# One decode step of attention and a squared-relu block: query tiles of 512 columns, output weights on VectorE, the bias behind the transposition

## The chip, the cores and the metric

The kernel runs on one core of a Trainium2 chip. The metric is the device time of one execution in microseconds, taken as the median of several runs. The kernel before ran at 1052.48 us (median of 3 runs, 1052.36 to 1053.69).

## What is computed

One token x of 640 values passes an attention block and a dense block, both modulated by a condition c:

```python
mod = (silu(c) @ w_mod)                      # six vectors: sa, ca, ga, sb, cb, gb
h = layernorm(x) * (1 + ca) + sa
q = (h @ wq)                                  # 32 heads of 192
p = softmax(q @ k_cache^T / sqrt(192))        # 8192 positions for each head
x = x + ga * ((p @ v_cache) @ wo)             # wo: 6144 x 640
h = layernorm(x) * (1 + cb) + sb
x = x + gb * (relu(h @ w1 + b1)**2 @ w2 + b2) # w1: 640 x 1536, w2: 1536 x 640
```

All is float32. The two caches are 403 MB of the 452 MB that are read, and each value is used once.

## The kernel before

The heads go in 16 pairs. A pair's keys come in three parts of 8192 values for each of the 128 partitions (64 positions a partition), its values in three parts of the same size. `ring` holds three slots; one transfer fills a slot with a part of keys (first half) and the part of values that is two parts older (second half). SyncE's queue is the order of all transfers: `l0` (the weights of the first modulation, the query weights of pairs 0 to 2, small columns), `l1` (query weights of pairs 3 to 10), `c0` and `c1` (the first key parts and the last query weights), 46 transfers of `stream`, and then `c48` (output weights of pairs 0 to 3 and values), `wob` (output weights of pairs 4 to 7), `wos` (of pairs 8 to 15), `c49` (the last values), `wm1`, `w1`, and `w2` in four pieces. `issue(n)` (lines 486 to 498) sends a transfer when the slot's keys are done (`tk_free`, from VectorE) and its values are done (`values_done`, from TensorE).

Ahead of the loops TensorE computes the query rows (lines 260 to 301): a round is up to four pairs, each pair's 384 columns in its own 32 rows of a PSUM bank, 5 contraction blocks. ScalarE copies them to `qr` (`keep_rows`). For each pair `act_stage` picks one pair's row into `stage`, a product with `ones` spreads it over all partitions (`pe_query`), and ScalarE copies that to `qb`.

Each engine then runs a loop of its own over the pairs. VectorE (`dve_pair`) multiplies a part of keys by the query in place, sums most of it, and finds the maximum; GpSimd adds the halves of the rest (line 385); ScalarE takes the exponential; TensorE (line 326) turns the pair's outputs before (`pe_turn`, line 324), multiplies values by probabilities in three steps of 16 units ("va", "vb", "vc"), spreads the next query between the first two, and sums the probabilities. TensorE's loop is created with `head_slot={ET.PE: 0}`: its first instruction is put at the start of a block of instruction memory.

Behind the loops VectorE multiplies the turned outputs by the output weights and adds them to `acc` (`attend`, line 449, three instructions of 640 columns for a pair) for pairs 0 to 13. It waits for `c48` (pairs 0 to 3), `wob` (4 to 7) and `wos` (8 and on). `project` (line 386) scales the last pair's outputs, head by head; `ON_DVE` is 14, so pair 13 comes behind the second head. TensorE takes pairs 14 and 15 itself, into `ps_att` (`pe_attend`, line 554), and then adds the sum of `acc` over the partitions to the same bank (line 570). The rest is one chain: gate and residual (lines 576, 577), layer norm with the second modulation's weights `wm1` between its steps on TensorE (line 193, called at 574, 580 and 585), a transposition (587), w1 (597), a transposition of the result (604), squared relu (605), w2 (615), gate, residual, and the transfer of the result. w1's bias enters ahead of w1 as four products with the identity (589); three more products with the identity (591) follow and their result isn't used.

Of the kernel before, what the change touches and what calls it, by code (L numbers as in the profile page):

```python
# [4 lines left out]
AF = mybir.ActivationFunctionType  # L5
ALU = mybir.AluOpType
# [3 lines left out]
P = 128  # L10
# [33 lines left out]
WM = KB * 3 * D  # L44
W2_CUT = (6 * D, 9 * D, 11 * D, FB * D)
GROUP = 4
ON_DVE = 14
EPS = 1e-5


# [47 lines left out]
        self.n = 0  # L98


def block_kernel(nc, l0, l1, c0, c1, stream, c48, wob, wos, c49, wm1, w1, w2, out):
    sem = nc.alloc_semaphore
    V, A, L, T, S = (Line(nc, e, n) for e, n in ((nc.vector, "dve"), (nc.scalar, "act"), (nc.gpsimd, "pool"),
                                                 (nc.tensor, "pe"), (nc.sync, "sp")))
# [11 lines left out]
    def sb(name, *shape):  # L116
        return nc.alloc_sbuf_tensor(name, [P, *shape], F32)
# [6 lines left out]
    ident, ones, mean = sb("ident", P), sb("ones", P), sb("mean", P)  # L124
    mask, quad, eps_t = sb("mask", E), sb("quad", NV), sb("eps_t", 1)
    small, e_t, h1 = sb("small", SMALL), sb("silu", KB), sb("h1", KB)
    qr, stage, qb = sb("qr", len(ROUNDS), PW), sb("stage", PW), sb("qb", PW)
    ga, x_t, bbt = sb("ga", DG), sb("x_t", DG), sb("bbt", 32 * (FB + KB))
    ra, rb, rc = sb("ra", NPOS), sb("rb", ROWS), sb("rc", NPOS)
    sc = [sb(f"sc{s}", NPOS) for s in range(2)]  # L130
    mp = [sb(f"mp{s}", 1) for s in range(2)]
# [10 lines left out]
    def dma(dst, src, s):  # L142
        nc.sync.dma_start(dst, src).then_inc(s, 16)  # L143
# [102 lines left out]
    def spread(dst, src, n):  # L246
        room = om[:, :, :].rearrange("p d e -> p (d e)")[:, :32 * n]
        V.wait(V.last())
        V.wait(V.mark(v.tensor_copy(room.rearrange("p (b r) -> p b r", r=32), src[:, :, None].to_broadcast([P, n, 32]))))
        V.mark(v.transpose(dst, room))  # L250

    spread(x_t[:, :], x_c, KB)
    spread(bbt[:, :32 * FB], bbc[:, :FB], FB)
    spread(bbt[:, 32 * FB:], bbc[:, FB:], KB)
    for a in range(2):
        V.mark(v.memset(ps_o[a][:96, :], 0.0))
    V.mark(v.memset(ps_sum[:, :2], 1.0))
    m_ready = V.last()

    def query_rows(r, w, bank):  # L260
        for b in range(KB):
            for g, i in enumerate(ROUNDS[r]):
                o = pe.matmul(bank[32 * g:32 * (g + 1), :PW], h1[:, b:b + 1].to_broadcast([P, 32]),
                              w[:, g * WQ + b * PW:g * WQ + (b + 1) * PW], start=(b == 0), stop=(b == KB - 1))
        return T.mark(o)

    def keep_rows(r, bank, m):
        A.wait(m)
        n = 32 * len(ROUNDS[r])
        return A.mark(act.activation(qr[:n, r], bank[:n, :PW], AF.Copy, scale=DH ** -0.5))  # L270

    def act_stage(i):
        r = [i in pairs for pairs in ROUNDS].index(True)
        g = ROUNDS[r].index(i)
        A.wait(m_rows[r])
        return act.activation(stage[:, :], qr[:, r], AF.Copy, scale=ident[:, 32 * g:32 * g + 1])

    def pe_query():
        return pe.matmul(ps_q[:, :PW], ones[:, :], stage[:, :], start=True, stop=True)
# [27 lines left out]
    def done(step, i):  # L307
        return T.sem, T0 + len(PE_STEPS) * i + PE_STEPS.index(step) + 1
# [13 lines left out]
    def pe_turn():  # L322
        T.take(tk_o)
        return pe.matmul(ps_oT[:, :NV], os_[:96].rearrange("p a d -> p (a d)"), quad[:96, :], start=True, stop=True)  # L324

    with nc.Fori(0, NPAIR, engines=bass.OrderedEngineSet([ET.PE]), head_slot={ET.PE: 0}):
        pe_turn().then_inc(T.sem, 1)
        pe_max(0)
        T.take(tk_c)
        T.take(tk_p[0])  # L330
        pe_values(2, range(16))
        T.take(tk_s)
        pe_query().then_inc(T.sem, 1)
# [56 lines left out]
    def project(a):  # L390
        n = 32 * NV
        return (v.scalar_tensor_tensor(om[:n], ps_o[a][:n].rearrange("p (d e) -> p d e", e=E), r2[:n, a:a + 1],  # L392
                                       mask[:n, None, :].to_broadcast([n, ED, E]), op0=ALU.mult, op1=ALU.mult),
                lambda: v.tensor_reduce(os_[:n, a], om[:n], axis=AX.X, op=ALU.add))  # L394
# [63 lines left out]

    def late_wo(i):
        group, k = divmod(i, GROUP)  # L460
        at = (slot[0], WO_AT) if group == 0 else (slot[1], 0) if group == 1 else (slot[2], (group - 2) * GROUP * WO)
        return at[0][:, at[1] + k * WO:at[1] + (k + 1) * WO]

    attended = {}
# [1 line left out]
    def attend_range(first, end, m):  # L466
        for i in range(first, end):
            attended[i] = attend(i, late_wo(i), m)
# [14 lines left out]
    def values_done(m):  # L483
        return done(("va", "vb", "vc")[m % 3], m // 3)
# [17 lines left out]
        forward(n)  # L502
        issue(n + 2)
    forward(PARTS - 1)
    S.wait((tk_free, PARTS - 1))
    dma(slot[1][:, :GROUP * WO], wob, w_sem[2])
    S.wait((tk_free, PARTS), values_done(PARTS - 3))
    dma(slot[2][:, :2 * GROUP * WO], wos, w_sem[3])
    S.wait(values_done(PARTS - 4))
    dma(slot[1][:, PART:], c49, slot_sem[1])  # L510
    forward(PARTS)

    attend_range(0, GROUP, landed(PARTS))
    attend_range(GROUP, 2 * GROUP, (w_sem[2], 16))
    V.wait(done("sum", NPAIR - 1))
    V.wait(V.mark(v.reciprocal(r2[:, :], ps_sum[:, :2])))
    for a in range(2):
        V.wait(done("vb" if a == 0 else "vc", NPAIR - 1))
        scaled, sums = project(a)
        V.wait(V.mark(scaled))  # L520
        o = sums()
        if a == 0:
            V.wait(V.mark(o))
            attend_range(2 * GROUP, ON_DVE - 1, (w_sem[3], 16))
        else:
            o.then_inc(tk_o, 1)
            attend_range(ON_DVE - 1, ON_DVE, (w_sem[3], 16))
    m_acc = attended[ON_DVE - 1]

    wm1_t, w1_t, w2_t = slot[0][:, :WM], slot[1][:, :KB * FF], slot[2][:, :FB * D]  # L530
    S.wait(done("vb", NPAIR - 1), attended[GROUP - 1])
    dma(wm1_t, wm1, w_sem[4])
    S.wait(attended[2 * GROUP - 1])
    dma(w1_t, w1, w_sem[5])
    forward(PARTS + 1)
    S.wait(attended[3 * GROUP - 1])
    a = 0
    for n, b in enumerate(W2_CUT):
        dma(w2_t[:, a:b], w2[:, a:b], w_sem[6 + n])
# [4 lines left out]
    def room(n):  # L544
        r = tail[0][:, :n]
        tail[0] = tail[0][:, n:]
        return r

    x1, gate, gb2, y, hT, cb1, xm2, sq2, h2 = (room(DG) for _ in range(9))
    f, fT = room(FG), room(FG)  # L550
    s2, ss2, sd2, rs2 = (room(1) for _ in range(4))
    ps_b, ps_f, ps_y = ps_mx[0], ps_o[0], ps_o[1]

    def pe_attend(i):
        wo = late_wo(i).rearrange("p (j n) -> p j n", j=NV)
        T.wait(turned[i])
        for j in range(NV):
            for g in range(G):
                o = pe.matmul(ps_att[32 * g:32 * (g + 1), :DG], oT[:, i, j:j + 1].to_broadcast([P, 32]),
                              wo[:, j, DG * g:DG * (g + 1)], start=i == ON_DVE and j == 0, stop=False)  # L560
        return o

    T.wait((w_sem[3], 16))
    for i in range(ON_DVE, NPAIR - 1):
        pe_attend(i)
    act_turned(NPAIR - 1, T.mark(pe_turn()))
    pe_attend(NPAIR - 1)
    T.wait(m_acc)
    for g in range(G):
        i = pe.matmul(ps_att[32 * g:32 * (g + 1), :DG], ones[:, :32], acc[:, DG * g:DG * (g + 1)], start=False, stop=True)  # L570
    m_att = T.mark(i)
    T.wait((w_sem[4], 16))
    w_b = wm1_t
# [11 lines left out]
                     lambda: mod(ps_b, w_b, 3, range(1, 3)), summed=True)  # L585
    V.wait(m_h2)
    m_hT = V.mark(v.transpose(hT, h2))
    for g in range(G):
        pe.matmul(ps_f[32 * g:32 * (g + 1), :FG], ident[:, 32 * g:32 * (g + 1)], bbt[:, :FG], start=True, stop=False)
    for _ in range(3):  # L590
        pe.matmul(ps_oT[:32, :512], ident[:, :32], bbt[:, :512], start=True, stop=True)
    T.wait(m_hT, (w_sem[5], 16))
    hT3 = hT.rearrange("p (b r) -> p b r", r=32)
    for b in range(KB):
        at = b * FF
        for g in range(G):
            i = pe.matmul(ps_f[32 * g:32 * (g + 1), :FG], hT3[:, b], w1_t[:, at + FG * g:at + FG * (g + 1)],
                          start=False, stop=(b == KB - 1))
    m_f = T.mark(i)
    V.wait(V.mark(v.tensor_copy(gate, ps_b[:, 2 * DG:3 * DG])))  # L600
    V.wait(V.mark(v.tensor_mul(gb2, gate, bbt[:, FG:])))
    m_x2 = V.mark(v.tensor_add(x1, x1, gb2))
    V.wait(m_f)
    V.wait(V.mark(v.transpose(f, ps_f[:, :FG])))
    m_fT = V.mark(v.scalar_tensor_tensor(fT, f, 0.0, f, op0=ALU.max, op1=ALU.mult))
    T.wait(m_fT)
    fT3 = fT.rearrange("p (b r) -> p b r", r=32)
    for b in range(FB):
        for n, c in enumerate(W2_CUT):
            if b * D < c:  # L610
                T.wait((w_sem[6 + n], 16))
                break
        for g in range(G):
            o = b * D + DG * g
            i = pe.matmul(ps_y[32 * g:32 * (g + 1), :DG], fT3[:, b], w2_t[:, o:o + DG], start=(b == 0), stop=(b == FB - 1))  # L615
    m_y = T.mark(i)
    V.wait(m_y, m_x2)
    V.wait(V.mark(v.tensor_mul(y, ps_y[:, :DG], gate)))  # L618
# [62 lines left out]
```

## Time and profile before

| | |
|---|---|
| median of 3 runs | 1052.48 us |
| the profiled execution | 1052.26 us, span 1050.9 us |
| VectorE busy | 868.7 us (83%) |
| TensorE matmul busy | 460.6 us (44%), 2154 matmuls |
| GpSimd busy | 193.4 us (18%) |
| ScalarE busy | 46.3 us (4%), 124 instructions |
| read from HBM | 451.82 MB, 430 GB/s over the span |

The span runs from the first to the last instruction of the execution that was profiled; its own time lies 1.4 us above it. A matmul of float32 is two passes, each with a load of weights, and the profile counts the passes. An engine that is busy for a small share of the span can still set the end if something waits for it there, so the shares are read beside the waits and the timeline.

### The profile page before, as it was taken

How to read it: one execution, taken by the hardware profiler on the slowest of the kernel's cores; microseconds unless marked ns; L12 is line 12 of the kernel's file. 1: busy time of each engine (PE TensorE's matmuls, PEld its weight loads, DVE VectorE, ACT ScalarE, POOL GpSimd, SP SyncE). 2: the span in 40 equal slices, each digit the busy share in tenths (PEclk: the TensorE clock that was granted, in tenths of full speed). 3: DMA queues.
4: the chain of work that ended last, by engine and by line, in shares of the span. 5: the costliest groups of instructions: out<-in, count | busy, mean ns of one | idle time of the engine just before them, and what ended most of it. 6: DMA issues, size and time to landing. Idle time of an engine off the chain costs nothing. (4 is left out here: it accounts for less than half of the span.)

```text
span 1050.9 us, 5797 instructions
## 1 busy us (share of the span) xinstructions
PE 460.6 (44%) x2154; PEld 142.4 (14%) x2154; DVE 868.7 (83%) x411; ACT 46.3 (4%) x124; POOL 193.4 (18%) x63
## 2 busy tenths in 40 slices
PE   1543444362543543453624434434526345344327
PEld 0211111110111111111101111111102011111103
DVE  0269999898889898998988897988988888979973
ACT  1100000000000000000000000000000000000000
POOL 1011313112122122131131121121211311311100
PEclk9966767666676666676676766666766767666759
DMA  9999999999999999999999999999999999999997
GB/s 412 417 434 440 437 437 437 434 434 417 439 437 437 437 432 437 419 437 437 437 439 427 439 424 432 437 439 437 432 434 427 429 439 437 437 437 432 421 429 333
DMA packets 8657, 451.92 MB, mean 430 GB/s; under 512 B 965, under 2 KB 969, under 8 KB 1353
## 3 DMA queue, kind: packets, MB, share of 16 engines
q1 hardware_dynamic: 8648, 451.83, 99.5%
q8 instruction: 4, 0.07, 0.0%
q14 instruction: 5, 0.03, 0.0%
HBM read 451.82 MB, written 0.00 MB: 430 GB/s over the span
## 5 line engine op out<-in xcount | busy, mean ns | idle before, releaser
L407 DVE TENSOR_TENSOR ring<-ring,qb 128x8192 f32<-128x8192 f32 x48 | 417.1, 8689 | 79.5 <-DVEq L84 79.5
L314 PE MATMUL ps_o<-ring,p 128*32 128x512 f32 x1536 | 357.9, 812 | 206.9 <-PEq L66 206.9
L385 POOL TENSOR_TENSOR ring<-ring 128x1792 f32<-128x1792 f32 x48 | 189.9, 3955 | 782.6 <-POOLq L66 782.6
L314 PEld LDWEIGHTS ps_o<-ring,p 128*32 128x32 f32 x1536 | 87.4, 144 | 453.2 <-issue 452.9
L320 PE MATMUL ps_mx<-ident,mp 128*128 128x128 f32 x64 | 24.5, 487 | 140.3 <-PEq L66 140.3
L324 PE MATMUL ps_oT<-quad,os 96*128 96x3 f32 x34 | 9.3, 344 | 169.1 <-PEq L66 169.1
L409 DVE TENSOR_REDUCE rc<-ring 128x36 f32<-128x4608 f32 x16 | 79.2, 4953 | 2.3
L409 DVE TENSOR_REDUCE ra<-ring 128x36 f32<-128x4608 f32 x16 | 79.2, 4953 | 2.3
L409 DVE TENSOR_REDUCE rb<-ring 128x72 f32<-128x4608 f32 x16 | 79.2, 4953 | 2.3
L454 DVE SCALAR_TENSOR_TENSOR acc<-ring,oT,acc 128x640 f32<-128x640 f32 x42 | 37.1, 884 | 4.9 <-DMA ring<-in_wos 2.7
L421 DVE TENSOR_REDUCE nm<-ps_mx 128x1 f32<-128x128 f32 x32 | 9.3, 291 | 34.1 <-DVEq L84 34.1
L320 PEld LDWEIGHTS ps_mx<-ident,mp 128*128 128x128 f32 x64 | 16.0, 311 | 150.6 <-issue 150.6
L324 PEld LDWEIGHTS ps_oT<-quad,os 96*128 96x128 f32 x34 | 8.3, 305 | 183.3 <-issue 183.3
L413 DVE TENSOR_REDUCE rc<-ring 128x28 f32<-128x1792 f32 x16 | 32.1, 2009 | 0.0
L413 DVE TENSOR_REDUCE ra<-ring 128x28 f32<-128x1792 f32 x16 | 32.1, 2009 | 0.0
L413 DVE TENSOR_REDUCE rb<-ring 128x56 f32<-128x1792 f32 x16 | 32.1, 2005 | 0.0
L354 ACT ACTIVATE oT<-ps_oT 128x3 f32<-128x3 f32 x16 | 2.8, 173 | 590.3 <-PE ps_oT L324 590.3
L392 DVE SCALAR_TENSOR_TENSOR om<-ps_o,r,mask 96x512 f32<-96x512 f32 x34 | 25.4, 747 | 3.8 <-PE ps_o L314 2.6
L347 ACT ACTIVATE p<-sc,nm 128x256 f32<-128x256 f32 x32 | 16.2, 508 | 185.8 <-DVE nm L421 185.8
L394 DVE TENSOR_REDUCE os<-om 96x64 f32<-96x512 f32 x34 | 23.2, 682 | 1.2
L336 PE MATMUL ps_sum<-sp,ones 128*128 128x2 f32 x32 | 8.9, 348 | 19.6 <-PEq L66 19.6
L193 PE MATMUL ps_o<-ring,silu 128*32 128x480 f32 x40 | 6.7, 837 | 23.1 <-DVE silu L186 23.1
(92 smaller groups left out, 153.8 us busy)
## 6 DMA issues: line engine op xcount, KB each, us to landing
ring<-in_c SPq DMA_DIRECT2D x2, 7936.0 KB, 48.2
ring<-in_l SPq DMA_DIRECT2D x1, 7693.5 KB, 21.2
ring<-in_l SPq DMA_DIRECT2D x1, 7680.0 KB, 38.9
ring<-in_wos SPq DMA_DIRECT2D x1, 7680.0 KB, 28.7
ring<-in_c SPq DMA_DIRECT2D x1, 5056.0 KB, 25.3
ring<-in_wm SPq DMA_DIRECT2D x1, 4800.0 KB, 36.5
ring<-in_c SPq DMA_DIRECT2D x1, 4096.0 KB, 38.1
ring<-in_wob SPq DMA_DIRECT2D x1, 3840.0 KB, 27.7
```

The source lines that it names most:

```text
L314: i = pe.matmul(ps_o[h][32 * g:32 * (g + 1), :], p_t[h][:, E * j:E * (j + 1)].rearrange("p e r -> p (e r)"), t[:, k], start=(j == 0), stop ...
L320: pe.matmul(ps_mx[s][:, :P], mp[s][:, :].to_broadcast([P, P]), ident[:, :], start=True, stop=True).then_inc(tk_x, 1)
L324: return pe.matmul(ps_oT[:, :NV], os_[:96].rearrange("p a d -> p (a d)"), quad[:96, :], start=True, stop=True)
L347: act.activation(p_t[s][:, :, :], sc[s][:, :, None].to_broadcast([P, NPOS, 32 // E]), AF.Exp, bias=nm[s][:, :], accum_out=sp[:, s:s + 1]). ...
L385: pool.tensor_add(r[:, keep:, :w], r[:, keep:, :w], r[:, keep:, w:]).then_inc(tk_fold, 1)
L392: return (v.scalar_tensor_tensor(om[:n], ps_o[a][:n].rearrange("p (d e) -> p d e", e=E), r2[:n, a:a + 1], mask[:n, None, :].to_broadcast([ ...
L394: lambda: v.tensor_reduce(os_[:n, a], om[:n], axis=AX.X, op=ALU.add))
L407: B.mark(v.tensor_mul(k, k, q))
L409: v.tensor_reduce(out[:, :keep], r[:, :keep], axis=AX.X, op=ALU.add)
L413: B.mark(v.tensor_reduce(out[:, keep:], r[:, keep:, :r.shape[2] // 2], axis=AX.X, op=ALU.add))
L421: v.tensor_reduce(nm[s][:, :], ps_mx[s][:, :P], axis=AX.X, op=ALU.max, negate=True).then_inc(tk_n, 1)
L454: V.mark(v.scalar_tensor_tensor(acc[:, :], w[:, j], oT[:, i, j:j + 1], acc[:, :], op0=ALU.mult, op1=ALU.add))
```

## The change

Query weights of a round stand side by side, and a round's columns are cut into tiles of 512 that may hold parts of two pairs: a full round has three products for each of 5 blocks in place of four. `keep_rows` and `act_stage` need two activations where a tile isn't full or a pair lies in two tiles. TensorE's loop loses its `head_slot`. The bias's spread over rows ahead of the loops goes; the bias is added to one column of the transposed result, and the squared relu then works on 12 columns. The transfers behind `c48` are cut in another way: `woa` (output weights of pairs 4 to 7, into the second half of slot 2), `wob` (of pairs 8 to 11, into its first half), and `c49` (of pairs 12 to 15 with the last values, into slot 1). `w1` goes to the second half of slot 2. All pairs' output weights are multiplied on VectorE: 8 to 11 ahead of the first head's projection, 12 and 13 between the two heads, 14 and 15 behind the second.

```diff
-ON_DVE = 14
+BANK = 512
...
     def query_rows(r, w, bank):
+        n = len(ROUNDS[r]) * PW
         for b in range(KB):
-            for g, i in enumerate(ROUNDS[r]):
-                o = pe.matmul(bank[32 * g:32 * (g + 1), :PW], h1[:, b:b + 1].to_broadcast([P, 32]),
-                              w[:, g * WQ + b * PW:g * WQ + (b + 1) * PW], start=(b == 0), stop=(b == KB - 1))
+            for g in range(0, n, BANK):
+                e = min(g + BANK, n)
+                o = pe.matmul(bank[32 * g // BANK:32 * g // BANK + 32, :e - g], h1[:, b:b + 1].to_broadcast([P, 32]),
+                              w[:, b * n + g:b * n + e], start=(b == 0), stop=(b == KB - 1))
...
     def act_stage(i):
         r = [i in pairs for pairs in ROUNDS].index(True)
-        g = ROUNDS[r].index(i)
+        at, end = ROUNDS[r].index(i) * PW, (ROUNDS[r].index(i) + 1) * PW
+        first = at
         A.wait(m_rows[r])
-        return act.activation(stage[:, :], qr[:, r], AF.Copy, scale=ident[:, 32 * g:32 * g + 1])
+        while at < end:
+            g, c = divmod(at, BANK)
+            n = min(end - at, BANK - c)
+            o = act.activation(stage[:, at - first:at - first + n], qr[:, r, c:c + n], AF.Copy,
+                               scale=ident[:, 32 * g:32 * g + 1])
+            at += n
+        return o
...
-    with nc.Fori(0, NPAIR, engines=bass.OrderedEngineSet([ET.PE]), head_slot={ET.PE: 0}):
+    with nc.Fori(0, NPAIR, engines=bass.OrderedEngineSet([ET.PE])):
...
-    S.wait((tk_free, PARTS - 1))
-    dma(slot[1][:, :GROUP * WO], wob, w_sem[2])
-    S.wait((tk_free, PARTS), values_done(PARTS - 3))
-    dma(slot[2][:, :2 * GROUP * WO], wos, w_sem[3])
-    S.wait(values_done(PARTS - 4))
-    dma(slot[1][:, PART:], c49, slot_sem[1])
+    S.wait(values_done(PARTS - 3))
+    dma(slot[2][:, PART:PART + GROUP * WO], woa, w_sem[2])
+    S.wait((tk_free, PARTS))
+    dma(slot[2][:, :GROUP * WO], wob, w_sem[3])
+    dma(slot[1][:, WO_AT:], c49, slot_sem[1])
     forward(PARTS)
...
+    attend_range(2 * GROUP, 3 * GROUP, (w_sem[3], 16))
+    V.wait(done("sum", NPAIR - 1), done("vb", NPAIR - 1))
     V.wait(V.mark(v.reciprocal(r2[:, :], ps_sum[:, :2])))
-    for a in range(2):
...
+    scaled, sums = project(0)
+    V.wait(V.mark(scaled))
+    V.mark(sums())
+    attend_range(3 * GROUP, NPAIR - 2, landed(PARTS + 1))
+    V.wait(done("vc", NPAIR - 1))
+    scaled, sums = project(1)
+    V.wait(V.mark(scaled))
+    sums().then_inc(tk_o, 1)
+    attend_range(NPAIR - 2, NPAIR - 1, landed(PARTS + 1))
+    act_turned(NPAIR - 1, T.mark(pe_turn()))
+    attend_range(NPAIR - 1, NPAIR, landed(PARTS + 1))
+    m_acc = attended[NPAIR - 1]
...
-    wm1_t, w1_t, w2_t = slot[0][:, :WM], slot[1][:, :KB * FF], slot[2][:, :FB * D]
+    wm1_t, w1_t, w2_t = slot[0][:, :WM], slot[2][:, PART:PART + KB * FF], slot[2][:, :FB * D]
...
-    S.wait(attended[2 * GROUP - 1])
+    S.wait(attended[3 * GROUP - 1])
     dma(w1_t, w1, w_sem[5])
     forward(PARTS + 1)
-    S.wait(attended[3 * GROUP - 1])
...
-    for i in range(ON_DVE, NPAIR - 1):
-        pe_attend(i)
-    act_turned(NPAIR - 1, T.mark(pe_turn()))
-    pe_attend(NPAIR - 1)
     T.wait(m_acc)
     for g in range(G):
-        i = pe.matmul(ps_att[32 * g:32 * (g + 1), :DG], ones[:, :32], acc[:, DG * g:DG * (g + 1)], start=False, stop=True)
+        i = pe.matmul(ps_att[32 * g:32 * (g + 1), :DG], ones[:, :32], acc[:, DG * g:DG * (g + 1)], start=True, stop=True)
...
-    for g in range(G):
-        pe.matmul(ps_f[32 * g:32 * (g + 1), :FG], ident[:, 32 * g:32 * (g + 1)], bbt[:, :FG], start=True, stop=False)
-    for _ in range(3):
-        pe.matmul(ps_oT[:32, :512], ident[:, :32], bbt[:, :512], start=True, stop=True)
+    for k in range(2):
+        pe.matmul(ps_oT[:32, :BANK], ident[:, :32], acc[:, k * P:k * P + BANK], start=True, stop=True)
...
     V.wait(V.mark(v.transpose(f, ps_f[:, :FG])))
-    m_fT = V.mark(v.scalar_tensor_tensor(fT, f, 0.0, f, op0=ALU.max, op1=ALU.mult))
-    T.wait(m_fT)
-    fT3 = fT.rearrange("p (b r) -> p b r", r=32)
+    f_c = f.rearrange("p (b r) -> p b r", r=32)[:, :, 0]
+    V.wait(V.mark(v.tensor_add(fc, f_c, bbc[:, :FB])))
+    m_fc = V.mark(v.scalar_tensor_tensor(fc, fc, 0.0, fc, op0=ALU.max, op1=ALU.mult))
+    T.wait(m_fc)
```

## Rows read from the trace of the kernel before

**Rows 1.** The page, busy share of the DMA engines in 40 slices.
```profile
DMA  9999999999999999999999999999999999999997
```

**Rows 2.** SyncE's own waits: us in total, times, longest us.
```profile
SPq L479 <- DMA ring<-in_stream: 854.4, 46, 18.8
```

**Rows 3.** Timeline, the query products ahead of the loops: start us, us, what.
```profile
32.56 3.42 PE L263 MATMUL ps_att<-ring,h 128*32 128x384 f32 x30 [1.43 <-DVE h L223]
...
40.10 6.66 PE L263 MATMUL ps_mx<-ring,h 128*32 128x384 f32 x80 [1.90 <-DMA ring<-in_l]
...
60.21 6.04 PE L263 MATMUL ps_att<-ring,h 128*32 128x384 f32 x40 [13.46 <-DMA ring<-in_c]
...
72.19 3.41 PE L263 MATMUL ps_mx<-ring,h 128*32 128x384 f32 x5 [5.94 <-DMA ring<-in_c]
```

**Rows 4.** Waits, ScalarE's exponential: us in total, times, longest us.
```profile
ACT p L347 <- DVE nm L421: 185.8, 32, 18.0
```

**Rows 5.** Timeline, transfers issued at the end.
```profile
979.68 0.33 SPq L143 DMA_DIRECT2D ring<-in_wos  x1
...
992.98 0.33 SPq L143 DMA_DIRECT2D ring<-in_wm  x1
...
1004.27 17.42 SPq L143 DMA_DIRECT2D ring<-in_w  x5
```

**Rows 6.** Timeline, last values and output weights.
```profile
972.63 0.91 PE L279 MATMUL ps_q<-stage,ones 128*128 128x384 f32 x2
...
981.67 3.72 DVE L454 SCALAR_TENSOR_TENSOR acc<-ring,oT,acc 128x640 f32<-128x640 f32 x4
...
1008.49 14.04 DVE L454 SCALAR_TENSOR_TENSOR acc<-ring,oT,acc 128x640 f32<-128x640 f32 x15 [2.67 <-DMA ring<-in_wos]
...
1018.29 6.35 PE L314 MATMUL ps_o<-ring,p 128*32 128x512 f32 x31 [27.99 <-PEq L66]
```

**Rows 7.** Timeline, the chain from the last projection to the end.
```profile
1026.49 2.71 DVE L454 SCALAR_TENSOR_TENSOR acc<-ring,oT,acc 128x640 f32<-128x640 f32 x3
...
1026.72 0.36 PE L324 MATMUL ps_oT<-quad,os 96*128 96x3 f32 x2 [0.83 <-PEq L66]
...
1029.26 0.48 PE L570 MATMUL ps_att<-acc,ones 128*32 128x160 f32 x8 [0.90 <-DVE acc L454]
...
1034.81 0.33 DVE L581 TENSOR_SCALAR ring<-ps_mx 128x160 f32<-128x160 f32 x1 [3.16 <-PE ps_mx L193]
...
1035.17 0.17 DVE L221 RECIPROCAL ring<-ring 128x1 f32<-128x1 f32 x1
...
1036.14 0.34 DVE L587 STREAM_TRANSPOSE ring<-ring 128x160 f32<-128x160 f32 x1
...
1038.74 3.43 PE L597 MATMUL ps_o<-ring 128*32 128x384 f32 x40 [0.80 <-DMA ring<-in_w]
...
1042.85 0.56 DVE L605 SCALAR_TENSOR_TENSOR ring<-ring 128x384 f32<-128x384 f32 x1
...
1043.46 1.84 PE L615 MATMUL ps_o<-ring 128*32 128x160 f32 x48 [1.29 <-DVE ring L605]
...
1047.14 1.26 PE L615 MATMUL ps_o<-ring 128*32 128x160 f32 x24 [0.50 <-DMA ring<-in_w]
```

**Rows 8.** Windows: stretch, us, busy PE, PEld, DVE, ACT, POOL, granted TensorE clock, DMA, GB/s.
```profile
66.00:69.00 3.00, 0.25 (x4) 0.00 (x0) 3.00 (x1) 0.49 (x1) 0.00 (x0) 0.99 1.00 431
69.00:72.00 3.00, 0.00 (x0) 0.00 (x0) 2.85 (x2) 0.00 (x0) 2.53 (x1) 0.50 1.14 494
964.00:967.00 3.00, 2.25 (x9) 0.66 (x12) 3.00 (x1) 0.60 (x2) 0.00 (x0) 0.50 1.22 529
967.00:970.00 3.00, 3.00 (x15) 0.80 (x12) 3.00 (x1) 0.00 (x0) 0.00 (x0) 0.50 1.03 444
1020.00:1022.00 2.00, 2.00 (x15) 0.64 (x12) 1.93 (x3) 0.00 (x0) 0.00 (x0) 0.68 0.98 422
```

**Rows 9.** DMA queues in 44:46, 130:980 and 980:1051: packets, MB, share of 16 engines.
```profile
q8 instruction: 1, 0.02, 3.1%
...
q14 instruction: 2, 0.02, 0.0%
...
q8 instruction: 2, 0.03, 0.2%
```

More of the change, by code (lines that the diff above doesn't have):

```diff
@@ L98, in close, with block_kernel @@
         self.n = 0
-def block_kernel(nc, l0, l1, c0, c1, stream, c48, wob, wos, c49, wm1, w1, w2, out):
+def block_kernel(nc, l0, l1, c0, c1, stream, c48, woa, wob, c49, wm1, w1, w2, out):
     sem = nc.alloc_semaphore
@@ L126, in block_kernel @@
     small, e_t, h1 = sb("small", SMALL), sb("silu", KB), sb("h1", KB)
-    qr, stage, qb = sb("qr", len(ROUNDS), PW), sb("stage", PW), sb("qb", PW)
-    ga, x_t, bbt = sb("ga", DG), sb("x_t", DG), sb("bbt", 32 * (FB + KB))
+    qr, stage, qb = sb("qr", len(ROUNDS), BANK), sb("stage", PW), sb("qb", PW)
+    ga, x_t, bbt = sb("ga", DG), sb("x_t", DG), sb("bbt", DG)
     ra, rb, rc = sb("ra", NPOS), sb("rb", ROWS), sb("rc", NPOS)
@@ L252, in block_kernel @@
     spread(x_t[:, :], x_c, KB)
-    spread(bbt[:, :32 * FB], bbc[:, :FB], FB)
-    spread(bbt[:, 32 * FB:], bbc[:, FB:], KB)
+    spread(bbt[:, :], bbc[:, FB:], KB)
     for a in range(2):
@@ L268, in keep_rows @@
         A.wait(m)
-        n = 32 * len(ROUNDS[r])
-        return A.mark(act.activation(qr[:n, r], bank[:n, :PW], AF.Copy, scale=DH ** -0.5))
+        n = len(ROUNDS[r]) * PW
+        for g in range(0, n, BANK):
+            if g == 0 or n - g < BANK:
+                rows, cols = (32 * (n // BANK), BANK) if n >= BANK and g == 0 else (32, n - g)
+                i = act.activation(qr[32 * g // BANK:32 * g // BANK + rows, r, :cols],
+                                   bank[32 * g // BANK:32 * g // BANK + rows, :cols], AF.Copy, scale=DH ** -0.5)
+        return A.mark(i)
     def act_stage(i):
         r = [i in pairs for pairs in ROUNDS].index(True)
-        g = ROUNDS[r].index(i)
+        at, end = ROUNDS[r].index(i) * PW, (ROUNDS[r].index(i) + 1) * PW
+        first = at
         A.wait(m_rows[r])
-        return act.activation(stage[:, :], qr[:, r], AF.Copy, scale=ident[:, 32 * g:32 * g + 1])
+        while at < end:
[5 more added lines that the diff above has]
+        return o
     def pe_query():
@@ L460, in late_wo @@
         group, k = divmod(i, GROUP)
-        at = (slot[0], WO_AT) if group == 0 else (slot[1], 0) if group == 1 else (slot[2], (group - 2) * GROUP * WO)
+        at = ((slot[0], WO_AT), (slot[2], PART), (slot[2], 0), (slot[1], WO_AT))[group]
         return at[0][:, at[1] + k * WO:at[1] + (k + 1) * WO]
@@ L514, in block_kernel @@
     attend_range(GROUP, 2 * GROUP, (w_sem[2], 16))
-    V.wait(done("sum", NPAIR - 1))
+    attend_range(2 * GROUP, 3 * GROUP, (w_sem[3], 16))
+    V.wait(done("sum", NPAIR - 1), done("vb", NPAIR - 1))
     V.wait(V.mark(v.reciprocal(r2[:, :], ps_sum[:, :2])))
-    for a in range(2):
[L518 to L528, printed above, removed]
-    wm1_t, w1_t, w2_t = slot[0][:, :WM], slot[1][:, :KB * FF], slot[2][:, :FB * D]
+    scaled, sums = project(0)
[11 more added lines that the diff above has]
+    wm1_t, w1_t, w2_t = slot[0][:, :WM], slot[2][:, PART:PART + KB * FF], slot[2][:, :FB * D]
     S.wait(done("vb", NPAIR - 1), attended[GROUP - 1])
     dma(wm1_t, wm1, w_sem[4])
-    S.wait(attended[2 * GROUP - 1])
+    S.wait(attended[3 * GROUP - 1])
     dma(w1_t, w1, w_sem[5])
     forward(PARTS + 1)
-    S.wait(attended[3 * GROUP - 1])
     a = 0
@@ L549, in block_kernel @@
     x1, gate, gb2, y, hT, cb1, xm2, sq2, h2 = (room(DG) for _ in range(9))
-    f, fT = room(FG), room(FG)
+    f, fc = room(FG), room(FB)
     s2, ss2, sd2, rs2 = (room(1) for _ in range(4))
     ps_b, ps_f, ps_y = ps_mx[0], ps_o[0], ps_o[1]
[L554 to L557, printed above, removed]
-            for g in range(G):
[L559 to L563, printed above, removed]
-    for i in range(ON_DVE, NPAIR - 1):
-        pe_attend(i)
-    act_turned(NPAIR - 1, T.mark(pe_turn()))
-    pe_attend(NPAIR - 1)
     T.wait(m_acc)
     for g in range(G):
-        i = pe.matmul(ps_att[32 * g:32 * (g + 1), :DG], ones[:, :32], acc[:, DG * g:DG * (g + 1)], start=False, stop=True)
+        i = pe.matmul(ps_att[32 * g:32 * (g + 1), :DG], ones[:, :32], acc[:, DG * g:DG * (g + 1)], start=True, stop=True)
     m_att = T.mark(i)
@@ L587, in block_kernel @@
     m_hT = V.mark(v.transpose(hT, h2))
-    for g in range(G):
-        pe.matmul(ps_f[32 * g:32 * (g + 1), :FG], ident[:, 32 * g:32 * (g + 1)], bbt[:, :FG], start=True, stop=False)
-    for _ in range(3):
-        pe.matmul(ps_oT[:32, :512], ident[:, :32], bbt[:, :512], start=True, stop=True)
+    for k in range(2):
+        pe.matmul(ps_oT[:32, :BANK], ident[:, :32], acc[:, k * P:k * P + BANK], start=True, stop=True)
     T.wait(m_hT, (w_sem[5], 16))
@@ L597, in block_kernel @@
             i = pe.matmul(ps_f[32 * g:32 * (g + 1), :FG], hT3[:, b], w1_t[:, at + FG * g:at + FG * (g + 1)],
-                          start=False, stop=(b == KB - 1))
+                          start=(b == 0), stop=(b == KB - 1))
     m_f = T.mark(i)
     V.wait(V.mark(v.tensor_copy(gate, ps_b[:, 2 * DG:3 * DG])))
-    V.wait(V.mark(v.tensor_mul(gb2, gate, bbt[:, FG:])))
+    V.wait(V.mark(v.tensor_mul(gb2, gate, bbt[:, :])))
     m_x2 = V.mark(v.tensor_add(x1, x1, gb2))
@@ L614, in block_kernel @@
             o = b * D + DG * g
-            i = pe.matmul(ps_y[32 * g:32 * (g + 1), :DG], fT3[:, b], w2_t[:, o:o + DG], start=(b == 0), stop=(b == FB - 1))
+            i = pe.matmul(ps_y[32 * g:32 * (g + 1), :DG], fc[:, b:b + 1].to_broadcast([P, 32]), w2_t[:, o:o + DG], start=(b == 0), stop=(b == FB - 1))
     m_y = T.mark(i)
@@ L648, with bulk @@
     wq = a(A_wq).reshape(G, KB, 32, NPAIR, PW).transpose(3, 0, 2, 1, 4).reshape(NPAIR, P, WQ)
+    def bulk(r):
+        w = wq[ROUNDS[r][0]:ROUNDS[r][-1] + 1].reshape(len(ROUNDS[r]), P, KB, PW)
+        return w.transpose(1, 2, 0, 3).reshape(P, len(ROUNDS[r]) * WQ)
     wo = a(A_wo).reshape(NPAIR, 2, NV, ED, D).transpose(0, 1, 3, 2, 4).reshape(NPAIR, P, WO)
@@ L661 @@
     arrays = {
-        "l0": join(rows(wm[:, :3 * D], KB), side(wq, 0, 3), column(A_x, KB), column(c, KB), column(B_b1, FB), column(B_b2, KB)),
-        "l1": side(wq, 3, 8),
-        "c0": join(kp[0], side(wq, 11, 4)),
-        "c1": join(kp[1], wq[15]),
+        "l0": join(rows(wm[:, :3 * D], KB), bulk(0), column(A_x, KB), column(c, KB), column(B_b1, FB), column(B_b2, KB)),
+        "l1": join(bulk(1), bulk(2)),
+        "c0": join(kp[0], bulk(3)),
+        "c1": join(kp[1], bulk(4)),
         "stream": np.concatenate([kp[LAG:], vp[:-LAG]], axis=2),
         "c48": join(side(wo, 0, GROUP), vp[-2]),
-        "wob": side(wo, GROUP, GROUP),
-        "wos": side(wo, 2 * GROUP, 2 * GROUP),
-        "c49": vp[-1],
+        "woa": side(wo, GROUP, GROUP),
+        "wob": side(wo, 2 * GROUP, GROUP),
+        "c49": join(side(wo, 3 * GROUP, GROUP), vp[-1]),
         "wm1": rows(wm[:, 3 * D:], KB),
```

## Prediction, made before the change was run

> **What bounds the kernel.** I read the page first: its slices show the DMA engines at nine tenths or more in all slices but the last [rows 1]. So time is the stream's bytes plus whatever follows the last landing. The DMA queue's own waits confirm it: SyncE spent 854.4 us in 46 waits for stream transfers to land [rows 2], next to nothing on freed buffers. An edit inside the stream counts only if it leaves the queue empty, adds bytes, or moves the end. Then I read the end in the timeline, from the last 64 value positions on. It holds a compute chain (weights' sums, layer norm, w1, w2) beside the last transfers (wm1, w1, w2), and at each joint the reader should ask which side came late. For w1 it was the transfer: TensorE waited 0.80 us for it at 1038.74. For w2 too: its third piece was waited for 0.50 us at 1047.14 [rows 7]. So the chain has room there: the transposed input of w1 was complete at 1036.14 + 0.34 = 1036.48, 2.26 us before w1.
>
> The sum is made against the profiled execution, 1052.26 us (span 1050.9 and 1.36 around it); the median of the three runs is 0.22 above it.
>
> **The start.** Each contraction block of a full round now is three products of 512 columns side by side instead of four of 384. Two rounds took 6.66 us [rows 3]; side by side the time goes by columns, so 6.66 x 512/384 = 8.88, 2.2 us more. Round 0 grows by up to a third of its 3.42 us, 1.1. So TensorE is done between 48.9 and 50.1 instead of 46.76. Behind it on SyncE stand c1 and the first stream transfer. The queue then still holds c0, which TensorE saw land at 60.21 [rows 3], so over 10 us of cover: 0. If that cover were gone, 2 to 3 us. Round 3 grows by a third too (6.04 to 8.1 us), but c1's product starts at 72.19 only [rows 3]: 0. VectorE's two instructions fewer before the loop are idle time: 0.
>
> **The loop.** Half of the pairs' query rows now straddle two tiles, so ScalarE stages them with two activations, each no longer than today's one. ScalarE waits 185.8/32 = 5.8 us on average for VectorE before each exponential [rows 4]: 0. [...]
>
> **The last transfers.** Bytes and number of transfers are the same: 3840, 3840 and 7936 KB behind c48 instead of 3840, 7680 and 4096. The first now waits for the value products in the second half of its slot, done at 972.63, where c48 had not landed before 981.67 [rows 6]; 9 us of cover for the time from issue to first byte, which no row shows: 0 as long as that is under 9. The two others leave when the last keys are free, 979.68 as before [rows 5]. wm1 is issued at 992.98 as now. w1 waits for pair 11 instead of pair 7, so its issue moves from 1004.27 to about 1015.6 (below), and w2 follows it at the landing of c49; c49 and wm1 are then still ahead in the queue, since w1's transfer ended at 1038.74: 0. The last landing stays where it is, bounds -0.5 to +0.5 for who shares which DMA engine.
>
> **VectorE at the end.** Fifteen products took 14.04 us, 0.94 each [rows 6]. Pairs 8 to 11 no longer wait for the 7680 KB that landed at 1008.49; their own half lands about 9 us earlier, so they run from 1004.3 to 1015.6, then the first head's projection to 1017.3. Pairs 12 and 13 need c49, whose value products start at 1018.29 [rows 6]: 1018.2 to 1023.9, before those products end near 1025. So far 0. But behind the second projection VectorE now does two pairs instead of one, because TensorE no longer takes 14 and 15: 1026.49 + 2 x 2.71 and a wait of 0.07 gives 1032.0, where it was 1029.2 [rows 7]. **+2.8 us** on the chain.
>
> **TensorE's clock.** In the same place TensorE loses its work: from the end of the turn, 1026.72 + 0.36 = 1027.1, to 1032.0 it does nothing, where it now has pair 15's products. No row shows this gap, so it is bounded by others. Below: the clock stays at its upper level, 0. Above: it falls, as it did where TensorE did 0.25 us of work in 66 to 69 and had 0.50 in 69 to 72 [rows 8]. I take the fall, since that gap is the nearest. How long the lower level lasts once work is back: from 1018.29 the clock was up after some 3.0 us (0.68 mean in 1020 to 1022), while 964 to 970 held 0.50 through 5.25 us of busy TensorE [rows 8]. Half of that stretch is lost, 1.5 to 2.6 us, as TensorE works through from 1029.26 to 1034.81 [rows 7], 5.5 us. The transposed input is then ready at 1036.48 + 2.8 + (1.5 to 2.6) = 1040.8 to 1041.9. That is 2.05 to 3.15 us behind today's start of w1.
>
> **w1 and w2.** From w1's start to w2's first product is 4.72 us today. The squared relu on 12 columns with the bias in an instruction of its own is two narrow instructions of 0.17 [rows 7] and a gap instead of 0.56: -0.15. The seven bias and warming products become two; they end beside the transposition as long as the clock is up: 0. So w2 starts at 1045.4 to 1046.5 instead of 1043.46. Its 96 matmuls take at most twice 1.84 = 3.7 us, by the smaller tail of each group nearer 3.5: done at 1048.9 to 1050.0, against 1047.14 + 1.26 = 1048.40 today. **+0.5 to +1.6, taken +1.0.** If the clock did not fall, w2 would start at about 1043.9 and end on its last landing: 0. So of the 2.8 us of the chain and the 2 us of clock, most vanishes in the 2.26 us before w1 and in the waits for w2.
>
> **Sum:** 1052.26 + 1.0 = 1053.3, and 0.22 for the median: 1053.5 us.
>
> **Rivals.**
> 1. The end stays on the last landing (clock up, or chain a little shorter): 1052.5. For it: two waits of TensorE for transfers in the tail. Against: the idle gap, and less slack than +2.8 needs.
> [...]
> 3. The clock doesn't come back before the end. Then 5.5, 3.43 and 3.5 us double: some 1063. Against: every stretch of steady work in this trace regained it.
> 4. Faster: the shorter program saves a fetch (1.0 us of one engine) just ahead of the last landing and the chain is hidden. At most -1.0: 1051.5; over 0.2% only with more that I can't name.
>
> **How the numbers follow.** 0.2% is 2.1 us, about what a measurement of this kernel can tell from no change. Chances: forecast 0.48, rival 1 0.19, rival 2 0.23, rival 3 0.06, rival 4 0.04. Within 0.2% lie rival 1, most of rival 4 and the forecast but for its late end: 0.65. Slower: rivals 2 and 3 and that end: 0.32. Faster: 0.03. The forecast's own range is 1052.7 to 1054.4. The whole one begins at rival 1's lower bound, 1052.0, and takes in the spread form of rival 2, 1057.5; its one-engine form and rival 3 stay out.
>
> **What would show it.** Right: L454 ending at 1032, L570 and the following products at a granted clock of 0.50 for 3 to 5 us, w1 no longer waiting for its transfer, w2's last matmuls without a wait for DMA, the stream's last landing unmoved. Wrong: dozens of packets on TensorE's instruction queue between 130 and 980; the clock at 1.00 through the gap; a hole in the DMA slices near 979.

## The result and the profile after

The changed kernel takes 1053.97 us (median of 22 runs, 1053.24 to 1054.77) beside 1052.36 us for the kernel before (22 runs, 1051.89 to 1053.72): 1.6 us more between the medians, and a ratio of 1.0014 with an interval of 1.0007 to 1.0020. That is less than the 0.2% which the prediction takes for about what a measurement can tell, but the interval lies clear of 1. Four of the 22 runs of the kernel before, at 1053.46 to 1053.72, took as long as the changed kernel; its trace is of a run of 1052.26 us, so why those four took longer isn't known. The profiled execution took 1053.73 us, its span is 1052.4, 1.5 above the span before.

The stream is as it was. On the page the DMA slices read as in [rows 1]; VectorE's products with the output weights are 48 instead of 42, and they wait 0.9 us for c49 where they waited 2.67 for wos [rows 6]:

```profile
DMA  9999999999999999999999999999999999999997
...
L467 DVE SCALAR_TENSOR_TENSOR acc<-ring,oT,acc 128x640 f32<-128x640 f32 x48 | 42.4, 884 | 3.5 <-DMA ring<-in_c 0.9
```

The time is behind it. The timeline of the changed kernel (start us, us, what) answers to [rows 5 to 7]; the first three lines are the issue of w1 and w2, the last value products, and pairs 14 and 15 on VectorE; line 193 is products with wm1:

```profile
1015.54 4.24 SPq L143 DMA_DIRECT2D ring<-in_w  x5
...
1018.09 6.64 PE L327 MATMUL ps_o<-ring,p 128*32 128x512 f32 x32 [28.07 <-PEq L66]
...
1026.15 5.54 DVE L467 SCALAR_TENSOR_TENSOR acc<-ring,oT,acc 128x640 f32<-128x640 f32 x6
...
1026.38 0.36 PE L337 MATMUL ps_oT<-quad,os 96*128 96x3 f32 x2 [1.65 <-PEq L66]
...
1031.75 0.76 PE L568 MATMUL ps_att<-acc,ones 128*32 128x160 f32 x8 [5.02 <-DVE acc L467]
...
1034.56 3.42 PE L193 MATMUL ps_mx<-ring,silu 128*32 128x480 f32 x16
...
1041.43 0.34 DVE L585 STREAM_TRANSPOSE ring<-ring 128x160 f32<-128x160 f32 x1
...
1041.84 3.43 PE L593 MATMUL ps_o<-ring 128*32 128x384 f32 x40
...
1046.38 3.47 PE L612 MATMUL ps_o<-ring 128*32 128x160 f32 x96 [1.12 <-DVE ring L603]
```

The reader is to see three things. Line 568, which adds up `acc`, starts at 1031.75 instead of 1029.26, and TensorE had been idle for 5.02 us. At the transposition (1041.43 instead of 1036.14) 5.3 us have been lost, 2.8 more than the 2.5 of that start: from line 568 to the transposition it is 9.68 us, where the kernel before took 6.88. And neither w1 (line 593) nor w2 (line 612) waits for a transfer any more: w2's 96 matmuls are one run of 3.47 us, which sets the end. The granted clock of the same stretch (columns as in [rows 8]):

```profile
1022.00:1024.00 2.00, 2.00 (x16) 0.60 (x11) 1.47 (x2) 0.00 (x0) 0.00 (x0) 1.00 1.00 426
...
1026.00:1028.00 2.00, 0.36 (x2) 0.30 (x2) 1.93 (x4) 1.21 (x2) 0.00 (x0) 0.90 0.86 369
1028.00:1030.00 2.00, 0.00 (x0) 0.00 (x0) 1.86 (x3) 0.24 (x1) 0.00 (x0) 0.50 0.93 399
1030.00:1032.00 2.00, 0.25 (x4) 0.20 (x8) 1.66 (x2) 0.00 (x0) 0.00 (x0) 0.50 1.07 461
1032.00:1034.00 2.00, 2.00 (x16) 0.39 (x8) 0.66 (x3) 0.00 (x0) 0.00 (x0) 0.50 0.96 415
1034.00:1036.00 2.00, 2.00 (x14) 0.90 (x14) 0.64 (x3) 0.00 (x0) 0.00 (x0) 0.50 0.93 399
1036.00:1038.00 2.00, 2.00 (x13) 0.29 (x5) 0.00 (x0) 0.00 (x0) 0.00 (x0) 0.54 0.92 392
1038.00:1040.00 2.00, 2.00 (x19) 0.84 (x20) 0.00 (x0) 0.26 (x1) 0.00 (x0) 1.00 1.08 461
```

It is 0.50, the lower of the two levels that the clock of this trace has (the other is 1.00), from 1028 to 1036, and 1.00 only from about 1038, when 24 of the 40 matmuls with wm1 are done. TensorE worked for some 6 us at the lower level; half of that, 3 us, agrees with the 2.8 that the 5.3 hold beyond the start. The instruction queue q8 (read as TensorE's: see the experiment with the loop pinned) has one packet in 117:124 and none in 130:980, where there are only two packets of another queue (q14), and two in 980:1053, both of them behind 1040, when the loop is over. In this order:

```profile
q8 instruction: 1, 0.02, 0.9%
...
q14 instruction: 2, 0.02, 0.0%
...
q8 instruction: 2, 0.03, 0.2%
```

### The profile page after: what moved, and what is told of

Read it like the earlier page. It is cut to its first block, busy times and chain, and to the rows that moved or that the text cites. A ratio compares the mean times of both kernels' runs of the same rounds, so it can differ in the third digit from the quotient of the medians.

```text
span 1052.4 us, 5634 instructions
## 1 busy us (share of the span) xinstructions
PE 456.6 (43%) x2066; PEld 139.4 (13%) x2066; DVE 872.8 (83%) x416; ACT 48.4 (5%) x133; POOL 194.0 (18%) x63
## 5 line engine op out<-in xcount | busy, mean ns | idle before, releaser
L327 PE MATMUL ps_o<-ring,p 128*32 128x512 f32 x1536 | 351.4, 798 | 208.5 <-PEq L66 208.5
L467 DVE SCALAR_TENSOR_TENSOR acc<-ring,oT,acc 128x640 f32<-128x640 f32 x48 | 42.4, 884 | 3.5 <-DMA ring<-in_c 0.9
L264 PE MATMUL ps_att<-ring,h 128*32 128x512 f32 (+1 forms) x60 | 11.4, 674 | 12.8 <-DMA ring<-in_c 11.4
```

The costliest lines, as they stand in the source:

```text
L264: o = pe.matmul(bank[32 * g // BANK:32 * g // BANK + 32, :e - g], h1[:, b:b + 1].to_broadcast([P, 32]), w[:, b * n + g:b * n + e], start=( ...
L327: i = pe.matmul(ps_o[h][32 * g:32 * (g + 1), :], p_t[h][:, E * j:E * (j + 1)].rearrange("p e r -> p (e r)"), t[:, k], start=(j == 0), stop ...
L467: V.mark(v.scalar_tensor_tensor(acc[:, :], w[:, j], oT[:, i, j:j + 1], acc[:, :], op0=ALU.mult, op1=ALU.add))
```

## Experiments

Each expectation names its theories; times are compared with runs of the kernel before on the same chip.

**Pairs 14 and 15 on TensorE again**, all other parts of the change kept. VectorE's order behind the loops is that of the kernel before too: pair 12 between the two heads, 13 behind the second.

```diff
+ON_DVE = 14
...
-    attend_range(3 * GROUP, NPAIR - 2, landed(PARTS + 1))
+    attend_range(3 * GROUP, ON_DVE - 1, landed(PARTS + 1))
...
-    attend_range(NPAIR - 2, NPAIR - 1, landed(PARTS + 1))
-    act_turned(NPAIR - 1, T.mark(pe_turn()))
-    attend_range(NPAIR - 1, NPAIR, landed(PARTS + 1))
-    m_acc = attended[NPAIR - 1]
+    attend_range(ON_DVE - 1, ON_DVE, landed(PARTS + 1))
+    m_acc = attended[ON_DVE - 1]
...
+    for i in range(ON_DVE, NPAIR - 1):
+        pe_attend(i)
+    act_turned(NPAIR - 1, T.mark(pe_turn()))
+    pe_attend(NPAIR - 1)
     T.wait(m_acc)
...
```

> The changed kernel with pairs 14 and 15 multiplied on TensorE again and pair 13 alone behind the second projection, all else as changed. Theory (the 1.5 us come from the two pairs behind the projection and from the idle gap that lowers TensorE's clock): the sum of the output weights is complete near 1029, the clock stays at 1.00, the transposed input of w1 is ready near 1036.5, w1 waits for its transfer again, and the time is that of the kernel before, ratio to it 0.9985 to 1.0005. Rival (the unpinned loop, the larger query tiles or the regrouped transfers cost it): the time stays with the changed kernel, ratio 1.001 to 1.002.

1052.27 us, ratio 0.9996 (0.9987 to 1.0005). The timeline has the old joints back, w1 behind its transfer and w2 behind its pieces:

```profile
1029.33 0.48 PE L581 MATMUL ps_att<-acc,ones 128*32 128x160 f32 x8 [0.90 <-DVE acc L468]
...
1036.20 0.34 DVE L598 STREAM_TRANSPOSE ring<-ring 128x160 f32<-128x160 f32 x1
...
1038.72 3.43 PE L606 MATMUL ps_o<-ring 128*32 128x384 f32 x40 [2.22 <-DMA ring<-in_w]
...
1043.31 1.84 PE L625 MATMUL ps_o<-ring 128*32 128x160 f32 x48 [1.16 <-DVE ring L616]
...
1047.08 1.26 PE L625 MATMUL ps_o<-ring 128*32 128x160 f32 x24 [0.52 <-DMA ring<-in_w]
```

So the larger query tiles, the second activations, the unpinned loop, the regrouped transfers and the bias behind the transposition cost nothing together, within that interval; the cost is in who multiplies pairs 14 and 15. This edit shortens VectorE's chain and fills TensorE's gap at once, so it doesn't part the two.

**The changed kernel with TensorE kept busy in the gap.**

```diff
+    for _ in range(5):
+        pe.matmul(ps_q[:32, :BANK], ident[:, :32], qr[:, 0], start=True, stop=True)
     T.wait(m_acc)
```

> The changed kernel with five products of no use (identity by query rows, 512 columns, into the bank of the spread query) on TensorE behind the last turn, so that it has about 4.3 us of work in the 4.7 us gap; the two pairs stay behind the projection. If the clock is what costs, granted clock 1.00 from 1022 on, the transposed input of w1 ready near 1039, w2's first product near 1043.9 and its last set by the last landing: ratio to the kernel before 0.999 to 1.0005. If the longer chain alone costs it, w2 ends near 1049.8 as in the changed kernel, ratio 1.001 to 1.002.

1052.51 us, ratio 0.9999 (0.9990 to 1.0008). In its timeline the sum starts at 1032.77, even later than in the changed kernel, yet the transposition comes 1.8 us earlier; the granted clock is 1.00 from 1026 to 1042, and 16 matmuls with wm1 take 1.82 us instead of 3.42. The line of PEld is the last load of weights for w2:

```profile
1027.68 4.48 PE L567 MATMUL ps_q<-qr,ident 128*32 128x512 f32 x10
...
1032.77 0.48 PE L570 MATMUL ps_att<-acc,ones 128*32 128x160 f32 x8 [0.60 <-DVE acc L467]
...
1034.37 1.82 PE L193 MATMUL ps_mx<-ring,silu 128*32 128x480 f32 x16
...
1039.65 0.34 DVE L587 STREAM_TRANSPOSE ring<-ring 128x160 f32<-128x160 f32 x1
...
1044.60 3.58 PE L614 MATMUL ps_o<-ring 128*32 128x160 f32 x96 [1.12 <-DVE ring L605]
...
1047.70 0.16 PEld L614 LDWEIGHTS ps_o<-ring 128*32 128x32 f32 x8 [0.23 <-DMA ring<-in_w]
```

The windows of the same kernel (columns as in [rows 8]):

```profile
1028.00:1030.00 2.00, 2.00 (x6) 0.55 (x5) 1.82 (x4) 1.26 (x1) 0.00 (x0) 1.00 0.96 415
1030.00:1032.00 2.00, 2.00 (x6) 0.33 (x3) 1.93 (x3) 0.00 (x0) 0.00 (x0) 1.00 1.03 445
1034.00:1036.00 2.00, 1.99 (x22) 0.71 (x18) 0.65 (x4) 0.00 (x0) 0.00 (x0) 1.00 0.97 415
```

With the same two pairs behind the projection, ten matmuls whose result nobody reads take the 1.5 us away. So with this chain the lower clock is what shows in the time. From the sum to the transposition it is 6.88 us, as in the kernel before; the lower clock made that 9.68. w2 waits for a transfer only ahead of its last load of weights, 0.23 us, and its 96 matmuls take 3.58 us instead of 3.47: the longer chain has used up the room to within some 0.1 us. No run has the converse, the lower clock without the longer chain. By an estimate from these rows it would cost nothing either: the transposed input would be ready at 1036.48 + 2.8 = 1039.3, and here it was ready at 1039.99 without a cost. So the 1.5 us are what the two make together beyond the room.

**TensorE's loop pinned again.**

```diff
-    with nc.Fori(0, NPAIR, engines=bass.OrderedEngineSet([ET.PE])):
+    with nc.Fori(0, NPAIR, engines=bass.OrderedEngineSet([ET.PE]), head_slot={ET.PE: 0}):
```

> The changed kernel with TensorE's loop at the start of a fetch block again. Theory: 16 KB fetches at other moments, no more than one of them more or fewer, and the time of the changed kernel, ratio to the kernel before 1.001 to 1.002. Rival (the loop's place costs the 1.5 us): ratio 0.9985 to 1.0005.

1053.94 us, ratio 1.0011 (1.0002 to 1.0020): the changed kernel's time, though the interval reaches down into the rival's range, so that the tail has to decide too. On q8 it has a packet in 81:87, where the changed kernel has none; the changed kernel had one in 117:124. The kernel before, with the pin too, has one in 81:84, between TensorE's last product ahead of the loop (over at 77.36) and the loop's first (93.44), and none in 84:130. Only TensorE's loop was edited here, which is why q8 is read as TensorE's queue. The DMA view of that stretch:

```profile
q8 instruction: 1, 0.02, 1.0%
```

The tail has the changed kernel's form, the idle gap and w2 in one run without a wait for DMA:

```profile
1032.55 0.76 PE L568 MATMUL ps_att<-acc,ones 128*32 128x160 f32 x8 [5.01 <-DVE acc L467]
...
1040.98 0.34 DVE L585 STREAM_TRANSPOSE ring<-ring 128x160 f32<-128x160 f32 x1
...
1045.92 3.47 PE L612 MATMUL ps_o<-ring 128*32 128x160 f32 x96 [1.11 <-DVE ring L603]
```

The lower level lasted less long here. The granted clock is 0.97 in 1036 to 1038, where the changed kernel had 0.54, and from the sum to the transposition it is 8.43 us, 1.55 above the 6.88:

```profile
1036.00:1038.00 2.00, 2.00 (x22) 0.69 (x18) 0.14 (x2) 0.13 (x1) 0.00 (x0) 0.97 0.90 376
```

**One pair left out.**

```diff
-    attend_range(NPAIR - 2, NPAIR - 1, landed(PARTS + 1))
     act_turned(NPAIR - 1, T.mark(pe_turn()))
```

> The changed kernel without pair 14's product with its output weights (left out of the sum), so that one pair stands behind the second projection, as before the change, and TensorE idles some 2 us there instead of 4.7. Theory: the sum is complete near 1029.0, and the clock decides the rest: if it stays up, w1 waits for its transfer and the ratio to the kernel before is 0.9985 to 1.0005; if it falls all the same, the input of w1 is ready near 1038.5 to 1039, w2 begins near 1043.5 and ends on its last landing, with about the same ratio. If the ratio stays at 1.001 or above, neither the chain nor the clock is the cause.

1053.15 us, ratio 1.0001 (0.9992 to 1.0010). The eleven runs fall into two groups, five at 1052.10 to 1052.48 and six at 1053.15 to 1053.86, so the median stands for neither. The ratio is in the expected range, but the expected tail wasn't met. In the profiled run (1053.57) the value products took 8.18 us instead of 6.64, pair 15 waited for the last turn, and the sum was complete at 1031.5, not 1029.0; the clock fell in a gap of 3.02 us. Its timeline:

```profile
1018.36 8.18 PE L327 MATMUL ps_o<-ring,p 128*32 128x512 f32 x32 [28.23 <-PEq L66]
...
1028.79 2.73 DVE L467 SCALAR_TENSOR_TENSOR acc<-ring,oT,acc 128x640 f32<-128x640 f32 x3 [0.74 <-ACT oT L367]
...
1031.57 0.76 PE L567 MATMUL ps_att<-acc,ones 128*32 128x160 f32 x8 [3.02 <-DVE acc L467]
```

Its windows (columns as in [rows 8]):

```profile
1022.00:1024.00 2.00, 2.00 (x9) 0.45 (x6) 1.73 (x2) 0.00 (x0) 0.00 (x0) 0.50 1.07 461
...
1030.00:1032.00 2.00, 0.43 (x8) 0.37 (x12) 1.48 (x2) 0.05 (x1) 0.00 (x0) 0.74 1.03 445
1032.00:1034.00 2.00, 2.00 (x17) 0.37 (x9) 0.66 (x3) 0.00 (x0) 0.00 (x0) 0.50 1.00 430
```

The value products were late because the granted clock was still 0.50 in 1022 to 1024, where the changed kernel had 1.00. So this run too came to the sum at the lower clock, behind 3.02 us of idle time. It doesn't part the chain from the clock, because both moved. What the five faster runs did isn't known, as the one trace is of a slower one.

**Nothing behind the projection.** Pairs 14 and 15 on TensorE as in the first experiment, and 12 and 13 both ahead of the second projection. The cut is against the first experiment.

```diff
-    attend_range(3 * GROUP, ON_DVE - 1, landed(PARTS + 1))
+    attend_range(3 * GROUP, NPAIR - 2, landed(PARTS + 1))
...
-    attend_range(ON_DVE - 1, ON_DVE, landed(PARTS + 1))
```

> The changed kernel with pairs 14 and 15 on TensorE and pairs 12 and 13 both ahead of the second projection, so that VectorE has no pair behind it; the sum waits for TensorE's own pair 15 only. Theory: the transposed input of w1 is ready about 1 us earlier than in the kernel before (near 1035.5), and nothing comes of it, since w1 and w2 wait for their transfers: ratio to the kernel before 0.9985 to 1.0005. Rival (the chain still sets the end of the kernel before): 0.9 us, ratio 0.999 or below with w2's products ending earlier.

1052.27 us, ratio 0.9999 (0.9990 to 1.0008). The sum starts 0.6 us earlier than in the kernel before, then waits for wm1 (0.42 us), and the transposition is where it was, at 1036.12 and not near 1035.5. So the chain did not get shorter, and the run doesn't tell what a shorter one would give. Its timeline:

```profile
1028.71 0.46 PE L580 MATMUL ps_att<-acc,ones 128*32 128x160 f32 x8
...
1029.59 1.01 PE L194 MATMUL ps_mx<-ring,silu 128*32 128x480 f32 x8 [0.42 <-DMA ring<-in_wm]
...
1036.12 0.35 DVE L597 STREAM_TRANSPOSE ring<-ring 128x160 f32<-128x160 f32 x1
...
1038.78 5.13 PE L605 MATMUL ps_o<-ring 128*32 128x384 f32 x40 [2.37 <-DMA ring<-in_w]
...
1045.02 3.47 PE L624 MATMUL ps_o<-ring 128*32 128x160 f32 x96 [1.11 <-DVE ring L615]
```

w1 took 5.13 us in place of 3.43: TensorE had been idle for 2.37 us ahead of it, where the kernel before filled the wait with seven products and this one has two, and the granted clock fell to 0.50 soon after w1 began. Its windows:

```profile
1038.00:1040.00 2.00, 1.22 (x12) 0.61 (x16) 0.00 (x0) 0.00 (x0) 0.00 (x0) 0.85 1.05 445
1040.00:1042.00 2.00, 2.00 (x16) 0.81 (x12) 0.00 (x0) 0.00 (x0) 0.00 (x0) 0.50 0.92 384
```

w2 began 1.56 us later than in the kernel before and ended 0.09 us later (1048.49 against 1048.40): the 1.7 us of w1 vanished in the waits for w2's pieces, and the time stayed.

**Three pairs behind, TensorE kept busy.**

```diff
-    attend_range(3 * GROUP, NPAIR - 2, landed(PARTS + 1))
+    attend_range(3 * GROUP, NPAIR - 3, landed(PARTS + 1))
...
-    attend_range(NPAIR - 2, NPAIR - 1, landed(PARTS + 1))
+    attend_range(NPAIR - 3, NPAIR - 1, landed(PARTS + 1))
...
+    for _ in range(8):
+        pe.matmul(ps_q[:32, :BANK], ident[:, :32], qr[:, 0], start=True, stop=True)
     T.wait(m_acc)
```

> The changed kernel with three pairs behind the second projection and eight products of no use on TensorE meanwhile, so that the clock stays up and the chain is 2.8 us longer than with two pairs and five such products. Theory: there w2 ended just as its last landing allowed, without a wait, so the room is used up and the 2.8 us come through in full: the input of w1 near 1042.5, the end of w2 near 1051, ratio to the kernel before 1.002 to 1.003. Rival (the end follows the landing whatever the chain does): ratio 0.9985 to 1.0005.

1055.08 us, ratio 1.0023 (1.0014 to 1.0032), 2.6 us above the kernel with two pairs behind and the clock kept up (1055.08 against 1052.51, each beside the kernel before on its own chip). Its timeline:

```profile
1036.05 0.48 PE L570 MATMUL ps_att<-acc,ones 128*32 128x160 f32 x8 [0.86 <-DVE acc L467]
...
1042.93 0.35 DVE L587 STREAM_TRANSPOSE ring<-ring 128x160 f32<-128x160 f32 x1
...
1047.88 3.47 PE L614 MATMUL ps_o<-ring 128*32 128x160 f32 x96 [1.12 <-DVE ring L605]
```

Against the trace with two pairs the transposition comes 3.28 us later (1042.93 against 1039.65) and w2 ends 3.17 us later (1051.35 against 1048.18). So once the room is gone the chain comes through nearly one for one. No version here beats the kernel before; three that compute the whole result reach its time.

## Why the prediction was right

- **The stream, the start, the loop: 0.** Right as far as the first experiment tells: with all of these parts in place the time was the one of the kernel before. The query products of two rounds side by side took 8.78 us (8.88 foretold). One reading was loose: beside the 854.4 us, SyncE waited for the query products ahead of c1 once for 44.7 us and for VectorE six times, 17.8 us in all, which is not next to nothing; the zero stood all the same, as the DMA slices stayed at nine tenths. w1's issue moved to 1015.54 (1015.6 foretold) and cost nothing.
- **VectorE, +2.8 us.** The sum started 2.5 us later (1031.75 against 1029.26). The two pairs took 5.54 us (5.42 foretold); VectorE came to them 0.3 us earlier than in the trace before (1026.15 against 1026.49). That was luck of this trace: with the same code up to there it was 1027.17 in the second experiment and 1026.96 in the third.
- **The clock, 1.5 to 2.6 us.** It fell as taken, and 0.50 lasted until about 1038, 6 us of work, more than either bound (3.0 and 5.25). The transposed input was ready at 1041.77, inside 1040.8 to 1041.9 only because the sum had come a little early. This bound is the weak step: the stretch at the lower level was bounded by two rows of other places, and here it came out longer than both. The term was sized at 2.0 in the middle and measured 2.8 in this trace (9.68 - 6.88); with the loop pinned again, the same tail, it measured 1.55. So its size differs from trace to trace, and that it came near the range is in part luck.
- **w1 and w2.** From w1's start to w2's first product 4.54 us (4.72 - 0.15 = 4.57 foretold), w2's first product at 1046.38 (1045.4 to 1046.5), its end 1.45 us behind the one before (1049.85 against 1048.40), in the range of 0.5 to 1.6, above the 1.0 taken. In the two traces the 1.5 us between the spans is this term and no other.
- **Rival 1** would have been right with the clock up: that is the second experiment. **Rival 2**, a cost of the loop's new place in TensorE's program, fell: no run shows the term behind the two forms that the range speaks of (1057.5, its upper end, for the spread one). What the trace shows is one packet on q8 in 117:124, while the loop's first pass runs (the value products of pair 0 behind 116.40), where the kernel before has none; in 130:980 there is none, and pinning the loop again gave nothing back (ratio 1.0011). **Rival 3** fell, the clock was back by about 1038 (1.00 in 1038 to 1040). **Rival 4** (its 1.0 us is the 3.1% of 16 engines in 2 us of [rows 9]) fell: q8 has four packets in either trace, and nothing ended earlier.

## What to carry to other kernels

Work that an engine does beside a chain can be worth more than its time: here TensorE's two pairs kept its clock up through the wait for VectorE (1.00 in 1026 to 1036 of the kernel before), and moving them cost the clock (0.50 in 1028 to 1036), 2.8 us of the chain in the trace, where the longer chain alone cost nothing (ratio 0.9999 with the clock kept up). What showed in the time was only the part of the two together that went beyond the room. Before a step is moved off TensorE, look at what TensorE will do in that gap, and price the stretch behind it at both levels of the clock, here 0.50 and 1.00. Where a stream sets the end, measure the room at each joint of the tail (who waits for whom); up to it a delay was free here (a transposition 3.51 us later in the second experiment, ratio 0.9999), beyond it a delay came through nearly in full (3.17 of 3.28 us in the last experiment).

## What the runs showed that was not expected

- Ahead of w1, in the kernel with nothing behind the projection, TensorE was idle for 2.37 us, and the granted clock fell to 0.50 within the first 2 us of w1 (5.13 us for 3.43 us of work). With 2.22 us at the same place, in the first experiment, it stayed up (3.43 us). So w1 ran at either level behind nearly the same wait.
- The last value products, the same code in all versions, took 6.64 us in the changed kernel's trace and 8.18 us in the one with a pair left out. The granted clock came up some 3 us later there (0.50 in 1022 to 1024, against 1.00), and VectorE's second projection started 1.8 us later (1026.58 against 1024.77). So two traces can differ ahead of the chain by more than the 1.5 us in question, and a tail is best read by intervals within one trace.
- TensorE's loop without its pin brought one packet on q8 in its 16 passes. The pages of the kernel before and of the changed kernel both show four packets on q8, 16 KB each (0.07 MB together); with the loop pinned one of them comes in 81:87, without the pin in 117:124, and the time doesn't show it (ratio to the kernel before 1.0011 with the pin, 1.0014 without).
